# Cluster attention then MoE attention on one core: rows of the first pair written from PSUM, causal mask and maximum in one instruction, and a new order table

## The chip, the cores and the metric

The kernel runs on one core of one Trainium2 chip. The metric is the device time of one execution in microseconds (us), as the median of several runs; less is better. A core has five instruction queues that matter here: PE (TensorE, matrix products and transposes), ACT (ScalarE), DVE (VectorE), POOL (GpSimd) and SP, which issues all of the kernel's DMAs. Each engine runs its own queue strictly in order. PE writes to PSUM, of which the kernel uses eight banks of 128 x 512 float32; ACT and DVE read and write PSUM and SBUF, POOL works in SBUF.

## The reference, cut to what matters

```python
def _attn_ref(q, k, v, centroids):              # B=4, H=8, S=768, D=64, 16 centroids
    q_assign = np.argmax(np.einsum('bhsd,hcd->bhsc', q_n, c_n), axis=-1)   # normalised
    k_assign = np.argmax(np.einsum('bhsd,hcd->bhsc', k_n, c_n), axis=-1)
    mask = q_assign[:, :, :, None] == k_assign[:, :, None, :]
    scores = np.where(mask, scale * np.matmul(q, k.transpose(0, 1, 3, 2)), -1000000000.0)
    ...                                          # softmax, then times v

def _moe_ref(x, w_gate, wq, wk, wv, wo):         # x: B, S, 512; E=4 experts; top 2
    logits = x @ w_gate
    topk = np.argpartition(-logits, K, axis=-1)[..., :K]
    ...                                          # w: softmax over the two chosen logits
    for e in range(E):
        q, k, v = x @ wq[e], x @ wk[e], x @ wv[e]
        causal = np.triu(np.ones((S, S), dtype=bool), 1)
        scores = np.where(causal, -1000000000.0, scale * (q @ k.transpose(0, 2, 1)))
        ...                                      # softmax a
        ye = a @ v @ wo[e]
        for kk in range(K):
            out += (topk[:, :, kk] == e)[..., None] * w[:, :, kk:kk + 1] * ye
```

Every query of the first part attends only to keys of its own cluster. The output of the first part, heads side by side, is the input x of the second, a causal attention per expert.

## The kernel before, in words

The work is cut into 24 sets. Sets 0 to 15 are pairs of heads of the cluster attention (four pairs for each of four batches); sets 16 to 23 are pairs of experts of the MoE attention, two for each batch. `K` and `Q` of a set are tiles `tk` and `tq` (three buffers each): for each of two heads, rows 0 to 63 hold the data split in a high and a low part of a float32, and the rows behind them extra rows that put a constant on the score. For a cluster set the rows 64 to 79 of K and Q are the **cluster rows**: a one-hot code of each token's cluster, on K's side scaled so that a key of another cluster gets minus 2^33. A product over 80 rows then gives scores that are already masked. Row 96 of Q holds minus the row maximum.

For a cluster set, `attention_operands` does: load q and k; PE transposes them (L531); PE multiplies them with the centroids `cbd` (L562), which are themselves made by `centroid_op` at the start (DVE's `cw`, L443; two transposes on PE, L449; a copy on ACT); PE transposes the result (L569); DVE makes the one-hot code `oh` in five instructions (L574, L575, L576, L581, L582); PE counts the clusters (L593); DVE drops with L600 those codes of q whose cluster no key has; PE transposes `oh` to rows (L607, into the bank `m4`); ACT scales them into the tile `rows` (L610); and two DMAs, `place_rows`, put them into K and Q. The product with `blk` on PE (L651) and DVE's L655, L659 and L663 zero the q of dropped codes. For the first set alone L655 and L659 write halves of Q directly instead of by DMA.

`core` then does, for each of two halves of the queries: the row scores (L978, PE, 80 rows, in float32), their maximum along the row (L988, DVE; partial maxima in `mx`, joined by L993), a transpose of the maxima (L1025 for the first set, L1004 otherwise) and a DMA or copy of them into row 96 of Q; then the transposed scores (L1059, L1060, PE), the exponential (L1065, ACT), the product with v (L1103, PE) and the sum of the exponentials for the norm, partly on POOL (L381) and partly on DVE (L382). For a MoE set the score tile of a query block ends with a 128x128 block on the diagonal: there DVE adds the mask `tri` to that block in PSUM (L986), and takes the maximum with L988. There are 96 such blocks, 12 in each of 8 sets, in tiles of 128 to 512 columns.

At the end of a MoE set the result of the product is copied from PSUM to a tile `avu` (two buffers; L376 on ACT or L377 on DVE), multiplied by the norm (`avu` by `rb`), copied as a high part into `kt` or `xk`, and the low part, `avu` minus `kt` or `xk`, is written to `qt` or `xq` (L381 on POOL or L382 on DVE). `moe_out` multiplies high and low part with the weights (L1213).

**What sets the order.** Each step is recorded as an operation, `op`, with a number. The table `SEQ` lists these numbers; `Plan.run` issues them in that sequence, so it fixes each engine's queue. A letter behind a number puts the operation on ACT, DVE or POOL instead of its first choice. `SLOT` fixes which of a tile's buffers each use takes. The durations and due times in `op(...)` play no part when the table is there. PE is kept busy at the start by matmuls of ones (`spin`, L1229).

## Time and profile before

| what | us |
|---|---|
| time, median of 3 runs | 701.75 (698.44 to 703.31) |
| the profiled execution's own time | 701.95 |
| span of the profiled execution, first to last instruction | 700.2 |
| mean granted TensorE clock | 0.996 of full speed |

The busy times are in rows 1 below. A stage is a stretch of the span: the start until the first row scores (about 21 us), the cluster stage to about 400 us, then the MoE stage, and a tail from 675 us. The chain of waits follows the work back from the last instruction to what released it; shares in it are shares of the span. A span counts as busy for PE whether the matmuls run at full clock or not, so the granted clock has to be read beside it.

### The profile page before, as it was taken

The page shows a single profiled execution, that of the slowest core. Times are in us where ns is not written, and L with a number is a line of the kernel's source. Part 1 is how long each engine was busy: PE and PEld are TensorE (multiplying, and loading weights), DVE is VectorE, ACT ScalarE, POOL GpSimd, SP SyncE. Part 2 cuts the span into 40 slices and gives each one's busy share as a digit, 9 for nine tenths or more (in the row PEclk, how much of TensorE's full clock was granted, in tenths as well). Part 3 has the DMA queues.
Part 4 walks back from the last instruction along what each step waited for, and adds up shares of the span by engine and source line. Part 5 has one row for each costly group of instructions (what it writes and reads, how often), then busy time and mean ns, then how long its engine had stood idle before and what let it go on. Part 6 is the DMA issues. An engine that isn't in the chain of part 4 may idle for free.

```text
span 700.2 us, 13106 instructions
## 1 busy us (share of the span) xinstructions
PE 680.8 (97%) x4523; PEld 526.6 (75%) x4523; DVE 554.7 (79%) x1215; ACT 350.5 (50%) x863; POOL 345.5 (49%) x285
## 2 busy tenths in 40 slices
PE   8999999999999999999999999999999989999997
PEld 6778767767767767767767688879779877877876
DVE  6998798888899688989999977783887766467842
ACT  5447545645645735656746532543452344333653
POOL 4585647479656387575486516134322236242221
PEclk9999999999999999999999999999999999999999
DMA  8766759678665777687859744537455455554223
GB/s 231 197 149 157 182 130 239 145 163 236 174 157 147 190 188 196 164 199 180 172 136 252 172 115 123 152 117 172 107 130 129 100 138 153 124 131 122 87 85 121
DMA packets 78094, 109.64 MB, mean 157 GB/s; under 512 B 22432, under 2 KB 61516, under 8 KB 78028
## 3 DMA queue, kind: packets, MB, share of 16 engines
q1 hardware_dynamic: 78028, 108.81, 62.0%
q8 instruction: 36, 0.59, 0.4%
q14 instruction: 30, 0.25, 0.1%
HBM read 36.54 MB, written 12.91 MB: 71 GB/s over the span
## 4 chain that ended last, share of the span: by engine, by line
PE 81%; DVE 9%; DMA 4%; issue 2%; ACT 1%; POOL 1%; SPq 1%; DVEq 0%; ACTq 0%; POOLq 0%
PE ps L1103 20%; PE ps L978 12%; PE ps L1059 11%; PE ps L1060 11%; PE ps L764 9%; PE ps L1213 5%; PE ps L816 4%; DVE mx L988 3%; PE ps L531 2%; PE ps L1127 2%; DMA tq<-mr 1%; DVE oh L582 1%; PE ps L562 1%; SPq L369 1%; DMA vt<-x 1%
## 5 line engine op out<-in xcount | busy, mean ns | idle before, releaser
L988 DVE TENSOR_REDUCE mx<-ps 128x1 f32<-128x384 f32 (+1 forms) x448 | 223.1, 544 | 24.6 <-PE ps L978 22.5
L1059 PE MATMUL ps<-tq,tk 128*128 128x384 f32 (+2 forms) x528 | 178.4, 341 | 1.2 <-ACT p L1065 1.2
L1060 PE MATMUL ps<-tq,tk 97*128 97x384 f32 (+2 forms) x528 | 173.7, 332 | 1.1 <-DMA tq<-mr 1.0
L1065 ACT ACTIVATE p<-ps 128x384 f32<-128x384 f32 (+2 forms) x288 | 119.2, 461 | 64.8 <-PE ps L1060 39.3
L978 PE MATMUL ps<-tk,tq 80*128 80x384 f32 (+4 forms) x512 | 144.9, 353 | 4.2 <-ACT avu L376 1.9
L1059 PEld LDWEIGHTS ps<-tq,tk 128*128 128x128 f32 x528 | 100.3, 190 | 10.3 <-issue 3.8
L978 PEld LDWEIGHTS ps<-tk,tq 80*128 80x128 f32 x512 | 89.4, 190 | 21.7 <-issue 9.1
L1060 PEld LDWEIGHTS ps<-tq,tk 97*128 97x128 f32 x528 | 100.6, 191 | 2.7 <-DMA tq<-mr 1.8
L381 POOL TENSOR_TENSOR acc<-acc,p 128x768 f32<-128x768 f32 (+2 forms) x37 | 58.2, 1574 | 63.3 <-DVE acc L382 26.2
L1070 POOL TENSOR_SCALAR_AFFINE_SELECT p<-p 128x256 f32<-128x256 f32 x48 | 21.6, 466 | 76.2 <-ACT p L1065 57.1
L1065 ACT ACTIVATE xl<-ps 128x384 f32<-128x384 f32 x88 | 40.7, 497 | 26.3 <-PE ps L1060 26.0
L1103 PE MATMUL ps<-p,vt 128*64 128x384 f32 x288 | 50.7, 491 | 0.0
L986 DVE TENSOR_TENSOR ps<-ps,tri 128x128 f32<-128x128 f32 x96 | 28.1, 292 | 22.4 <-PE ps L978 22.3
L381 POOL TENSOR_TENSOR acc<-p,p 128x768 f32<-128x768 f32 (+1 forms) x11 | 19.3, 1754 | 50.6 <-ACT p L1065 34.0
L376 ACT ACTIVATE hi<-ps 128x384 fp32r<-128x384 f32 x38 | 18.6, 492 | 48.6 <-PE ps L764 38.9
L1103 PE MATMUL ps<-p,vm 128*64 128x384 f32 (+2 forms) x288 | 41.5, 423 | 0.0
L1065 ACT ACTIVATE xh<-ps 128x384 f32<-128x384 f32 x80 | 37.8, 498 | 5.2 <-PE ps L1060 4.7
L382 DVE TENSOR_TENSOR acc<-acc,p 128x768 f32<-128x768 f32 (+2 forms) x33 | 26.8, 811 | 14.8 <-POOL acc L381 7.7
L1103 PEld LDWEIGHTS ps<-p,vt 128*64 128x64 f32 x288 | 19.6, 136 | 23.7 <-issue 21.4
L1178 POOL TENSOR_TENSOR xt<-avu,rb 128x384 f32<-128x384 f32 x26 | 26.6, 1035 | 15.7 <-DMA rb<-rd 15.7
L988 DVE TENSOR_REDUCE M<-ps 128x1 f32<-128x512 f32 (+3 forms) x64 | 31.4, 491 | 2.2
L1103 PEld LDWEIGHTS ps<-p,vm 128*64 128x64 f32 x288 | 18.5, 136 | 19.1 <-issue 13.5
(271 smaller groups left out, 1447.6 us busy)
## 6 DMA issues: line engine op xcount, KB each, us to landing
tq<-hi SPq DMA_DIRECT2D x88, 192.0 KB
tk<-hi SPq DMA_DIRECT2D x60, 192.0 KB
tk<-lo SPq DMA_DIRECT2D x46, 192.0 KB
rb<-rd SPq DMA_DIRECT2D x46, 192.0 KB
tq<-lo SPq DMA_DIRECT2D x45, 192.0 KB
vt<-in_v_dram SPq DMA_DIRECT2D x16, 384.0 KB
x<-xt SPq DMA_DIRECT2D x16, 384.0 KB
tk<-hi SPq DMA_DIRECT2D x16, 384.0 KB
```

The lines of the kernel that those rows point to most:

```text
L381: ways = [("pool", t_pool(n), lambda: POOL.tensor_tensor(dst(), a(), b(), op=fn)), ("dve", t_dve(n), lambda: DVE.tensor_tensor(dst(), a(), ...
L382: ("dve", t_dve(n), lambda: DVE.tensor_tensor(dst(), a(), b(), op=fn))]
L764: PE.matmul(m()[:, :HW], w_()[:, dc, es], x_[dc]()[:, c], start=(i == 0), stop=(i == 3 * DC - 1))
L816: PE.matmul(m()[:, :NV], x_[dc]()[:, ts], w_()[:, dc, :], start=(i == 0), stop=(i == 3 * DC - 1))
L978: PE.matmul(ps()[:, :w], Q[0:R, 0, h, c * 128:(c + 1) * 128], K[0:R, 0, h, i * w:(i + 1) * w], start=True, stop=True)
L986: DVE.tensor_tensor(e, e, tri, op=OP.add)
L988: DVE.tensor_reduce(to, ps()[:, :w], axis=AX.X, op=OP.max)
L1059: PE.matmul(p()[:, o_:HW], K[:, 1, h, ks], Q[:, 1, h, qs], start=True, stop=False)
L1060: PE.matmul(p()[:, o_:HW], K[0:R, 0, h, ks], Q[0:R, 0, h, qs], start=False, stop=True)
L1065: ACT.activation(pt()[:, h, o_:HW], p()[:, o_:HW], AF.Exp, scale=SC)
L1103: PE.matmul(av()[h * 64:(h + 1) * 64, o_:HW], d["vv"](h, kc), pt()[:, h, o_:HW], start=(kc == 0), stop=(kc == nk - 1), tile_position=(0, 6 ...
L1213: PE.matmul(m(), a_()[:, ts], w_()[:, ep, :], start=(ep == 0 and i == 0), stop=(ep == EP - 1 and i == 2))
```

## The change

**The first set's rows.** For set 0 the codes of `oh` are laid out head by head, so that `m4` holds 16 rows together for each of K and Q and each head. For the first half of the tokens (384 columns) these rows go from `m4` into K (new L635, DVE, or L639, ACT) and into Q (new L642, ACT, or L644, DVE): four instructions of 16 x 384. The other halves go by four small DMAs. L600's two instructions of 96 columns become four of 48 (new L608). `blk` for set 0 becomes `blk0`, which is made at the start from a shift, `pj`, one more DVE instruction there; `blk` itself is made later.

**Mask and maximum.** `tri` becomes 512 columns wide: 384 of zeros (one more memset on DVE) and the old triangle. A diagonal tile of w columns gets one `tensor_tensor_reduce`: sum of the tile and the last w columns of `tri`, written back to PSUM, and its maximum. In the queue it stands as two rows, the operation and a read of the accumulator (both new L1018). Other tiles keep the plain maximum (new L1020).

**The table.** `SEQ` and `SLOT` are new throughout. The gate's small tiles `gt` and `gs` take the tags `oh` and `sm`. Counts change little: PE 3320 to 3321 rows, DVE 1195 to 1188, ACT 855 to 866, POOL 270 to 276, SP 399 to 393.

```diff
 SEQ = """
-0 39 1 48 2 221 3 245 230 4 5 33 34 44 63 40 45 49 41 42d 389 46 37 50 51 38 47 68 6 52 7 43 54 66 55 8 9 67 10 56
...
-    tri = consts.tile([128, 128], BF)
-    DVE.tensor_scalar(tri, jp, 0.0, -BIG, op0=OP.is_gt, op1=OP.mult)
+    tri = consts.tile([128, 512], BF)
+    DVE.memset(tri[:, :384], 0.0)
+    DVE.tensor_scalar(tri[:, 384:], jp, 0.0, -BIG, op0=OP.is_gt, op1=OP.mult)
...
+    pj = sb.tile([128, 2, 128], I32, name="p1_0")
+    DVE.tensor_scalar(pj, pi, 4, None, op0=OP.arith_shift_right)
...
-        DVE.tensor_tensor(blk, pi, di, op=OP.is_equal)
+        DVE.tensor_tensor(blk0, pj, di, op=OP.is_equal)
...
         def ohg():
+            if n == 0:
+                return oh().rearrange("p a (i g c) -> p (a i) g c", i=2, c=NK)
...
-            for par in range(2):
+            for h in range(4 if n == 0 else 0):
+                w, cnt = oh()[:, :, h * NK:(h + 1) * NK], m3()[:, None, h // 2 * NK:(h // 2 + 1) * NK]
+                DVE.scalar_tensor_tensor(w, cnt.to_broadcast([128, HC, NK]), 1.0, w, op0=OP.min, op1=OP.mult)
+            for par in range(2 if n else 0):
...
+        for h in range(0 if n else 2):
+            def go_d(h=h):
+                DVE.tensor_scalar(K[64:64 + NK, 0, h, :HW], m4()[64 + 32 * h:64 + 32 * h + NK, :HW], BIG, -BIG,
+                                  op0=OP.mult, op1=OP.add)
...
+            half_row[h].append(op("dve", t_dve(HW), go_d, c2 + 6.6, [o4] + free, [m4], alt=("act", t_act(HW) + 0.18, go_a)))
+            half_row[h].append(op("act", t_act(HW), lambda h=h: ACT.activation(
+                Q[64:64 + NK, 0, h, :HW], m4()[32 * h:32 * h + NK, :HW], AF.Copy), c2 + 6.7, [o4] + free, [m4],
...
+            def place(T, i, h=h):
+                r = 64 * i + 32 * h + NK
+                return lambda: dma(T[64:64 + NK, 0, h, HW:], rows()[r:r + NK])
+            need_row.append(op("sp", [(0.64, 0.25)], place(K, 1), c2 + 7, [o_r] + free, [rows]))
+            need_row2.append(op("sp", [(0.64, 0.25)], place(Q, 0), c2 + 15, [o_r] + free, [rows]))
...
-                PE.matmul(m()[:, :HW], blk[:, h], rows(), start=True, stop=True)
-            o = op("pe", t_mm(HW), go, due, [o_r], [m, rows])
+                PE.matmul(m()[:, :HW], (blk if n else blk0)[:, h], rows(), start=True, stop=True)
+            o = op("pe", t_mm(HW), go, due, [o_r] + ([blk_ready] if n == 1 else []), [m, rows])
...
-        t, s, wt = tmp("gt", (128, 3, NC, E)), tmp("gs", (128, 6, NC)), tmp("wt", (128, E, NC))
+        t, s, wt = tmp("oh", (128, 3, NC, E)), tmp("sm", (128, 6, NC)), tmp("wt", (128, E, NC))
...
+                    to = mx()[:, h, cc, i:i + 1] if nb == 2 else tops(h)[:, cc:cc + 1]
                     if moe and i == nb - 1:
-                        e = ps()[:, w - 128:w]
-                        DVE.tensor_tensor(e, e, tri, op=OP.add)
-                    to = mx()[:, h, cc, i:i + 1] if nb == 2 else tops(h)[:, cc:cc + 1]
-                    DVE.tensor_reduce(to, ps()[:, :w], axis=AX.X, op=OP.max)
+                        DVE.tensor_tensor_reduce(ps()[:, :w], ps()[:, :w], tri[:, 512 - w:], 1.0, -3.0e38, OP.add, OP.max, to)
+                    else:
+                        DVE.tensor_reduce(to, ps()[:, :w], axis=AX.X, op=OP.max)
```

Three places show what the table moves. The first is PE's queue at the start, where the transposes of set 0's k and q (L531, new L535) meet those of the centroids (L449, new L453, reading `avu`). Before:

```order
L531 MATMUL ps_168<-identf,kt_142 128x128 x3
L531 MATMUL ps_176<-identf,kt_142 128x128 x3
L531 MATMUL ps_182<-identf,qt_146 128x128 x3
L449 MATMUL ps_192<-identf,avu_72 128x128 x2
L531 MATMUL ps_197<-identf,qt_146 128x128 x3
```

With the change:

```order
L535 MATMUL ps_174<-identf,kt_146 128x128 x3
L453 MATMUL ps_182<-identf,avu_72 128x128 x2
L535 MATMUL ps_187<-identf,kt_146 128x128 x3
L535 MATMUL ps_194<-identf,qt_150 128x128 x3
L535 MATMUL ps_201<-identf,qt_150 128x128 x3
```

The transposes of the centroids move ahead by two places: three of the four groups for k and q now stand behind them, where one did.

The second is DVE's queue from the end of set 0's one-hot code to the zeroing of q (before L582 to L655; with the change L588 to L687); `xh` and `xk` there belong to the second set. Before:

```order
L582 TENSOR_TENSOR oh_268<-ps_227,sm_237 128x6x4x16
L377 COPY xh_0_257<-ps_241 128x384
L600 SCALAR_TENSOR_TENSOR oh_268<-ps_283,oh_268 128x3x32 x2
L382 TENSOR_TENSOR xh_0_298<-xh_0_257,xh_0_272 128x384
L377 COPY xk_308<-ps_245 128x384
L377 CAST hi_316<-ps_245 128x384
L655 TENSOR_TENSOR tq_103<-xq_195,ps_322 64x384
L659 TENSOR_TENSOR tq_103<-xq_195,ps_322 64x384
L663 TENSOR_TENSOR xq_195<-xq_195,ps_322 128x384
```

With the change:

```order
L588 TENSOR_TENSOR oh_269<-ps_232,sm_240 128x384
L608 SCALAR_TENSOR_TENSOR oh_269<-ps_281,oh_269 128x3x16 x4
L377 COPY xh_0_300<-ps_257 128x384
L635 TENSOR_SCALAR tk_106<-ps_302 16x384
L644 CAST tq_107<-ps_302 16x384
L687 TENSOR_TENSOR tq_107<-xq_205,ps_317 64x384
L691 TENSOR_TENSOR tq_107<-xq_205,ps_317 64x384
L695 TENSOR_TENSOR xq_205<-xq_205,ps_317 128x384
```

Two copies of the second set (`xk` and `hi`) and one subtraction left this stretch, and the two rows of set 0 that DVE writes itself stand in it.

The third is in the MoE stage, near 560 us of the trace, where a set ends: the subtraction that writes `xq` from `avu` and `xk`, and the copy of a later product into the same buffer of `avu` (its second buffer, `avu_1`). Before, the subtraction is on POOL, between additions to `acc`:

```order
L1070 AFFINE_SELECT p0_0_7424<-p0_0_7424 128x2x128
L381 TENSOR_TENSOR acc_0_7517<-p3_0_7380,p0_0_7424 128x2x256
L381 TENSOR_TENSOR xq_0_7520<-avu_1_6849,xk_0_7370 128x768
L381 TENSOR_TENSOR acc_1_7614<-p2_0_7433,p3_0_7556 128x768
L381 TENSOR_TENSOR acc_1_7614<-acc_1_7614,p0_0_7542 128x768
```

With the change the subtraction is on DVE:

```order
L1018 ISA M6_113 128x1
L1018 ISA ps_6_7373,M6_113<-ps_6_7373,tri_80 128x128
L1018 ISA M6_113 128x1
L1020 TENSOR_REDUCE mx_0_7375<-ps_3_7371 128x1
L382 TENSOR_TENSOR xq_0_7403<-avu_1_6942,xk_0_7331 128x768
```

The copy into that buffer is then on DVE too (before it was on ACT), 27 rows behind the subtraction:

```order
L1018 ISA ps_1_7491,M6_113<-ps_1_7491,tri_80 128x384
L1018 ISA M6_113 128x1
L377 COPY avu_1_7524<-ps_2_7514 128x384
L1020 TENSOR_REDUCE mx_0_7375<-ps_1_7526 128x1
L1018 ISA ps_6_7535,M6_113<-ps_6_7535,tri_80 128x512
```

Over the MoE stage's seven such subtractions of qt and xq, POOL has five before and one with the change; the others are DVE's.

## Rows read from the trace of the kernel before

**Rows 1.** Two lines of the profile's page: the busy time of each engine (share of the span, number of instructions), and the chain that ended last, by engine.

```profile
PE 680.8 (97%) x4523; PEld 526.6 (75%) x4523; DVE 554.7 (79%) x1215; ACT 350.5 (50%) x863; POOL 345.5 (49%) x285
...
PE 81%; DVE 9%; DMA 4%; issue 2%; ACT 1%; POOL 1%; SPq 1%; DVEq 0%; ACTq 0%; POOLq 0%
```

**Rows 2.** Busy time by stage: the start, the rest of the cluster stage, the MoE stage, the tail. Columns: from:to (us), length, busy us and instructions of each engine, granted TensorE clock, share of the DMA engines, GB/s.

```profile
0.00:21.00 21.00, 18.17 (x138) 13.00 (x138) 15.58 (x46) 9.88 (x20) 10.38 (x20) 1.00 0.82 221
21.00:400.00 379.00, 372.15 (x2479) 273.15 (x2480) 336.90 (x686) 217.90 (x518) 240.12 (x164) 1.00 0.73 178
400.00:675.00 275.00, 269.55 (x1777) 224.21 (x1776) 194.25 (x469) 113.59 (x308) 91.45 (x98) 0.99 0.49 126
675.00:700.00 25.00, 20.93 (x134) 16.20 (x132) 8.02 (x16) 9.09 (x18) 3.53 (x4) 0.97 0.31 111
```

**Rows 3.** The chain that ended last, from the start to 27 us. Columns: start us, us, what.

```profile
7.02 0.28 PE ps L449 x2
7.30 0.33 PE ps L531 x3
...
16.17 0.55 DVE tq L655
...
18.96 0.55 DVE xq L663
...
22.84 2.65 DVE mx L988 x6
...
25.80 0.57 PE ps L1025 x3
```

**Rows 4.** The timeline from 13 to 21 us. Columns: start us, us, engine, line, operation, out<-in.

```profile
13.48 0.58 DVE L377 COPY xh<-ps 128x384 f32<-128x384 f32 x1
...
15.69 0.44 PE L651 MATMUL ps<-rows,blk 128*128 128x384 f32 x1
15.70 0.62 SPq L369 DMA_DIRECT2D tk<-rows  x1
...
16.41 1.27 SPq L369 DMA_DIRECT2D tq<-rows  x1
...
20.93 0.41 PE L978 MATMUL ps<-tk,tq 80*128 80x384 f32 x1 [0.68 <-DMA qt<-in_q_dram]
```

**Rows 5.** The timeline from 2 to 7 us, the setup of constants on DVE and POOL. Columns as in rows 4.

```profile
2.19 0.33 DVE L425 TENSOR_SCALAR acc<-acc 128x256 int32<-128x256 int32 x1
...
2.44 0.76 POOL L467 MEMSET tk<- 64x768 f32 x1
2.45 0.90 DVE L426 TENSOR_SCALAR acc<-acc 128x256 int32<-128x256 int32 x1
...
3.27 0.21 DVE L434 SCALAR_TENSOR_TENSOR avu<-rb 128x64 f32<-128x64 f32 x1
...
6.11 0.73 DVE L443 TENSOR_SCALAR avu<-rb,nr 128x64 f32<-128x64 f32 x2
```

**Rows 6.** DVE's instructions grouped by line, operation and tile, over the whole span, a group for each shape. Columns: line, operation, out<-in, shapes, number, busy us, mean ns of one, idle before.

```profile
L600 DVE SCALAR_TENSOR_TENSOR oh<-ps,oh 128x96 bf16<-128x96 f32 x32 | 6.9, 261 | 1.1 <-PE ps L593 0.8 <-issue 0.2
...
L395 DVE MEMSET avu<- 128x256 f32 x1 | 0.3, 272 | 0.0
...
L434 DVE DVE_READ_ACCUMULATOR avu<-rb 128x1 f32 x1 | 0.1, 78 | 0.0
```

**Rows 7.** The same view of DVE, for the mask, a row maximum of 512 columns, and a product of 384 columns with one input in PSUM.

```profile
L986 DVE TENSOR_TENSOR ps<-ps,tri 128x128 f32<-128x128 f32 x96 | 28.1, 292 | 22.4 <-PE ps L978 22.3
...
L663 DVE TENSOR_TENSOR xq<-xq,ps 128x384 f32<-128x384 f32 x30 | 15.7, 547 | 3.4 <-PE ps L651 3.3
...
L988 DVE TENSOR_REDUCE M<-ps 128x1 f32<-128x512 f32 x16 | 11.1, 692 | 0.5
```

**Rows 8.** What DVE waited for from 400 to 700 us. Columns: engine, tile, line, what it waited for: us in total, times, longest us.

```profile
DVE ps L986 <- PE ps L978: 22.3, 19, 5.2
```

**Rows 9.** The same view of what PE waited for from 400 to 700 us.

```profile
PE ps L1004 <- DVE M L993: 0.7, 1, 0.7
```

**Rows 10.** Busy time in 2 us windows around 562 us, columns as in rows 2.

```profile
560.00:562.00 2.00, 0.11 (x2) 0.04 (x1) 1.93 (x4) 0.58 (x2) 1.39 (x1) 1.00 0.98 252
562.00:564.00 2.00, 2.00 (x6) 1.84 (x7) 1.93 (x6) 1.66 (x5) 0.00 (x0) 0.51 0.64 143
564.00:566.00 2.00, 2.00 (x10) 1.62 (x9) 0.66 (x2) 0.49 (x3) 0.00 (x0) 0.64 0.01 3
```

**Rows 11.** The chain that ended last, 559 to 563 us, columns as in rows 3.

```profile
559.63 1.77 POOL xq L381
...
561.42 0.50 ACT avu L376
...
561.96 0.65 PE ps L978
```

**Rows 12.** One instruction of DVE in the timeline from 559 to 562 us, columns as in rows 4.

```profile
559.79 1.63 DVE L853 TENSOR_TENSOR gt<-gt,gs 128x24 f32<-128x24 f32 x1
```

**Rows 13.** DVE's instructions by shape: the subtraction of the MoE output's high part, and an addition of 128x768, both with two inputs in SBUF.

```profile
L382 DVE TENSOR_TENSOR wvh<-xl,xl 128x768 f32<-128x768 f32 x1 | 2.3, 2333 | 0.0
...
L382 DVE TENSOR_TENSOR xq<-avu,xk 128x768 fp32r<-128x768 f32 x1 | 1.0, 960 | 0.3 <-ACT xk L376 0.3
```

**Rows 14.** POOL's instructions by shape: the same subtraction there.

```profile
L381 POOL TENSOR_TENSOR xq<-avu,xk 128x768 fp32r<-128x768 f32 x2 | 3.6, 1822 | 0.0
```

More of the change, by code (lines that the diff above doesn't have):

```diff
@@ L222 @@
+    vt="110000010101010100101010100110",
+    mx="0101010101101001100110101001011001010101",
     ssb="01010101010101010101010",
[L223 removed]
+    acc="010101010101010101010110101010100101",
     avu="010101010101010101010101",
     r="0101010101010101010101010",
[L226 removed]
+    xt="0100100110100010010010101001011010110",
     mr="01010101010101010101010",
[L228 removed]
+    vm="011010110101",
     lg="0101",
[L230 removed]
+    g="01230123",
@@ L1233 @@
     cbd_ready = centroid_op()
+    blk_ready = op("dve", 0.33, lambda: DVE.tensor_tensor(blk, pi, di, op=OP.is_equal), base(0) + 10, at=4.9)
     POOL.memset(MZ, 0.0)
```

379 lines of the change are left out of this document (195 added, 184 removed), and 6 rows, old and new, of the table SEQ.

## The prediction

> **What bounds the kernel now.** I read the busy times and the engines' shares of the chain first. PE is busy for 680.8 of 700.2 us, and 81% of the chain is PE; DVE holds 9% of it, though it is busy for 79% of the span [rows 1]. So an instruction saved on DVE is worth its time only where PE waits for it, and the next view has to say where PE is idle. By stages PE is idle for 2.83 of the first 21 us, 6.85 of the next 379, 5.45 of the 275 of the MoE stage, and 4.07 of the tail [rows 2]. That is all there is to win without taking work off PE, and the change takes none off. DVE is idle for 275 − 194.25 = 80.75 us of the MoE stage [rows 2].
>
> Then the chain at the start. Until 16 us it goes through PE (transposes, centroids) and DVE's one-hot code; from 16.17 us it lies on DVE alone: product and zeroing of q for two heads until 19.51, then the second pair's one-hot code, then six row maxima from 22.84 to 25.49, and only then PE again [rows 3]. The first row score starts at 20.93 [rows 4], some 2 us before DVE takes its maximum: the DMAs of the rows, which this change partly removes, are not what the chain waits for there.
>
> Then the one place in the MoE stage where PE stands still. [...] The chain there is POOL's subtraction `xq` (1.77 us), then ACT's copy into the `avu` that this subtraction reads, then a row score [rows 11].
>
> **The change part by part**, against the profiled execution's 701.95 us; that lies 0.2 above the median of the runs, 701.75.
>
> *Setup.* Two DVE instructions are added ahead of the centroids' norm, which starts right behind L426 on a full queue [rows 5]: a memset, at most the 0.27 us of one of 128x256 float32 [rows 6], and a shift of 128x256 integers, like L425 (0.33) or like L426 (0.90, while a POOL memset runs) [rows 5]. That is 0.60 to 1.17 us later for `cw`, or nothing if the load of the centroids is what the norm waits for. I take 0.6, since the norm started only as L426 ended. `cw` was done at 6.84 [rows 5], and its transposes began at 7.02 [rows 3], so there was 0.18 us in hand.
>
> *Transposes.* PE now takes the centroids' transposes second, with three groups of k and q behind them instead of one; a group took 0.33 and the centroids' pair 0.28 [rows 3]. They end at 6.84 + 0.6 + 0.28 + 3 × 0.33 = 8.71 instead of 7.63: +1.1. Bounds: 8.11 with no delay of `cw` (+0.5), 9.28 with 1.17 (+1.65). PE is in order, and nothing but ones stands there to fill the gap.
>
> *Strips.* Two instructions of 0.261 [rows 6] become four of half the columns. If the time went by columns alone, nothing is added; if not at all, 2 × 0.261 = 0.5. I take +0.2. The start is then +1.3 (bounds +0.5 and +2.15).
>
> *Rows from PSUM.* Two 16 x 384 instructions on DVE and two on ACT. Their bound is a 384-column instruction on DVE, 0.55 each [rows 7]. They go where DVE had the second pair's copies, in the time in which PE transposes, ACT makes `rows` and PE makes the first product at 15.69 [rows 4]; I cost them at nothing. If that cover were short, at most 1.1 us would be added. The gain is nothing too: the maxima still stand behind the second pair's one-hot code on DVE (the order's second place), so scores that come earlier only wait. What the DMA's share was in front of the first score is 20.93 − 16.72 = 4.2 us [rows 3, 4]; that is the first rival.
>
> *Mask and maximum.* 96 mask additions of 0.292 go [rows 7], and 96 accumulator reads come at 0.078 [rows 6]: 28.0 − 7.5 = 20.5 us less on DVE, if the joined instruction takes as long as the maximum did. Two rows speak for that: a product of 384 columns with one input in PSUM takes 0.547, and from the mask's 0.292 at 128 columns to a maximum's 0.692 at 512 it is 1.04 ns a column with 0.16 fixed [rows 7]. If instead it ran at half that rate, 31,744 columns (1,984 for each head of a set, 2 heads, 8 sets) would add 33 us, and DVE would do some 12.5 us more than now; the stage's 80.75 idle us cover that. On the path: DVE waits 22.3 us for scores before the mask [rows 8], so it is mostly ahead of PE here. PE waited for joined maxima once, for 0.7 us [rows 9]. I take −0.5; bounds: 0, and −1.5 if as much again goes elsewhere.
>
> [...]
>
> *Stall at 560 us.* PE lost 1.89 us there, and by the granted clocks 0.49 × 2 + 0.36 × 2 = 1.70 behind it [rows 10]: 3.6 in all. With the change that `xq` is on DVE, where it takes 0.96 instead of 1.82 [rows 13, 14], and it stands 27 rows ahead of the copy that waits for it, so POOL's queue (an addition to `acc` just ahead of it) no longer holds the copy. I take −3.6. What is late next there is DVE itself, which had its own queue full at 559 to 562 us [rows 10].
>
> *All else of the table.* PE's rows are the same work; DVE gets a few more subtractions in the MoE stage (six of seven instead of two), 4 × 0.96 = 3.8 us [rows 13], less than what the masks give back. I cost that at nothing.
>
> Sum: 701.95 + 1.3 − 0.5 − 3.6 = 699.15, so **699.2**. With all bounds of these terms: 701.95 + 0.5 − 1.5 − 3.6 = 697.35 to 701.95 + 2.15 − 3.6 = 700.5.
>
> **The rivals.**
>
> *The stall stays or moves* (702.75): 699.15 + 3.6. Two buffers of `avu`, in-order queues, and a new sequence: another wait of 2 us with its half clock behind it can arise at any of the seven set ends. For it: one such place was there, and the order alone doesn't tell when DVE reaches the subtraction. Against it: the stage has only one such place in 275 us. It also stands for the case that the table doesn't do what it seems to.
>
> *The start follows the rows* (695.0): if the first maxima could be taken as the first scores come, 4.2 us less: 699.15 − 4.2 = 694.95. For it: this is where the change puts the most new code. Against it: the chain from 16.17 to 25.5 is DVE's, and DVE's order there has the same work.
>
> *PE's idle time in the MoE stage goes* (695.7): all 5.45 us and the 1.70 of half clock instead of −0.5 and −3.6: 701.95 + 1.3 − 5.45 − 1.70 = 696.1, with setup at its lower bound 695.3; middle 695.7. For it: DVE has 20 us more room. Against it: DVE wasn't what most of these waits ended with [rows 9].
>
> *Subtractions on DVE held by POOL* (709.95, slower). Four subtractions with two inputs in SBUF move to DVE. An addition of 128x768 of that kind took 2.33 us once on DVE instead of 0.95 [rows 13], and an instruction of 24 columns with two inputs in SBUF took 1.63 us, from 559.79, while POOL's `xq` ran from 559.63 to 561.40 [rows 11, 12]. So DVE can be held as long as POOL's instruction lasts, and behind such a subtraction stand maxima and copies that PE waits for. If three of the four do to PE what happened at 560, at 3.6 each: 699.15 + 10.8 = 709.95. One is the first rival over again; it decides the sign from three on. Against it: POOL's five subtractions of 1.82 us leave, and such holding is there today without a stall of PE but one.
>
> [...]
>
> **How the numbers follow.** Chances: forecast 0.42, stall stays or moves 0.24, start 0.12, MoE idle 0.10, held subtractions 0.12. The likeliest is 699.2. The range from 693 to 706 takes in all but the last case and leaves room below for two of the gains together and above for a second stall (702.75 + 3.6 = 706.35). About 1% (7 us) is what a measurement of this kernel can tell from no change: 694.7 to 708.8. Faster by more: the start and MoE cases when they come with the low setup or together, 0.18 with a part of the forecast's lower tail. Slower by more: the held subtractions, 0.12. Within: 0.70.
>
> **What would show it.** Right: the centroids' transposes (new L453) begin at about 7.4 us and the first zeroing of q about 1.3 us later than 16.17; the joined instruction and its read together take about 0.77 us at 512 columns; the masks leave PE's share of the chain as it is; no window of the MoE stage has PE at 0.1 busy and a half clock. Wrong: a first transpose of the maxima much before 25.8 us (the rows did count); an idle PE before a copy into `avu` elsewhere (moved stall); DVE subtractions of 2 us ahead of late maxima (held). The cluster stage, where the table changes as much and for which I cost nothing, could prove the sum incomplete in either direction: its 6.85 us of PE idle bound the gain there, nothing bounds a loss.

## The result, and the profile after

The changed kernel takes 704.99 us (median of 16 runs, 701.04 to 710.74), the kernel before 701.08 (16 runs, 698.44 to 703.31). The ratio is 1.0059 with a 95% interval of 1.0038 to 1.0080: about 4 us slower, where 699.2 and a gain of 2.5 us had been forecast. By the 1% that a measurement was said to tell it is "no change", but the sign is beyond the interval. The runs of the changed kernel scatter twice as widely as those of the kernel before, and the profiled execution is the slowest of the 16, 710.74 us (span 709.0), so its losses are larger than those of the median run; e3 below shows one place where the scatter comes from. Ratios below are to runs of the kernel before on the same chip.

Two lines of the changed kernel's page, busy times and the engines' shares of the chain (compare [rows 1]):

```profile
PE 688.9 (97%) x4523; PEld 531.4 (75%) x4523; DVE 528.2 (74%) x1210; ACT 354.3 (50%) x873; POOL 354.3 (50%) x289
...
PE 81%; DVE 11%; DMA 3%; ACT 2%; issue 1%; SPq 0%; POOL 0%; DVEq 0%; ACTq 0%; POOLq 0%
```

Its busy times by stage, columns as in [rows 2]:

```profile
0.00:21.00 21.00, 17.03 (x111) 11.78 (x111) 12.45 (x43) 7.67 (x14) 12.36 (x23) 1.00 0.62 182
21.00:400.00 379.00, 370.36 (x2471) 271.49 (x2468) 327.12 (x671) 219.62 (x525) 251.51 (x170) 0.99 0.71 176
400.00:675.00 275.00, 272.50 (x1776) 225.90 (x1777) 176.69 (x476) 116.79 (x313) 83.82 (x91) 0.98 0.50 130
675.00:700.00 25.00, 23.89 (x151) 18.35 (x150) 11.26 (x22) 7.79 (x20) 6.64 (x8) 0.93 0.20 70
```

DVE works 17.6 us less from 400 to 675 us (176.69 for 194.25), and PE is idle there for 2.50 us instead of 5.45: that part of the plan came true. PE's share of the chain is the same 81%. The start lost (PE idle for 3.97 us instead of 2.83), and so did the rest of the cluster stage (8.64 instead of 6.85). The granted clock is lower in three stages: 0.99, 0.98 and 0.93 where it was 1.00, 0.99 and 0.97. Over the whole span PE is busy for 688.9 us instead of 680.8, with the same 4,523 instructions: by the profile most of the 8.8 us by which this span is longer than that of the kernel before are longer instructions of PE, not its waits.

What PE waited for, over the whole span: engine, tile, line, what it waited for, us in total, times, longest.

```profile
PE ps L1091 <- ACT xk L376: 2.6, 1, 2.6
...
PE ps L453 <- DVE p L448: 2.3, 1, 2.3
PE ps L1036 <- DVE M L1018: 1.7, 1, 1.7
PE ps L1092 <- DMA tq<-mr: 1.6, 1, 1.6
...
PE ps L928 <- DVE acc L382: 1.1, 1, 1.1
```

The kernel before had one wait above 1.5 us outside the start, the 1.9 us at 560 us [rows 10, 11]. That one is gone. In this execution four stand in its place: for ACT's `xk` (at 164 us), for DVE's maxima (at 523), for the DMA of the maxima `tq<-mr` (at 398) and for DVE's `acc` (at 689); and one in the start, for the centroids (the row names L448, but the transposes read `avu`, which L447 wrote until 7.66). By the traces of the experiments below they aren't equally firm. The one at 164 us is 2.5 us or more wherever it isn't repaired, and the one for `acc` 1.1 to 1.4 us wherever it isn't repaired, except in e1; the one at 398 us is 0.4 to 1.9 us long, and the one at 523 us, 1.7 us here, is at most 1.2 us elsewhere and mostly small or absent.

**The start.** The chain, columns as in [rows 3]:

```profile
7.68 0.69 PE ps L453 x2
8.37 1.92 PE ps L535 x9
...
11.14 1.44 PE ps L568 x8
...
14.02 0.57 DVE sm L580
...
18.36 0.68 ACT rows L621
...
19.07 0.02 DVEq L635
...
19.13 0.56 DVE tk L635
...
19.71 0.55 DVE tq L644
...
20.29 0.55 DVE tq L687
...
23.73 0.48 DVE sm L580
```

The centroids' transposes (new L453) start at 7.68 us, 0.66 later than before [rows 3]. But they take 0.69 instead of 0.28, and the three groups behind them 0.64 each instead of 0.33. By these durations PE runs at about half speed until past 13 us, and it did so ahead of its wait of 2.3 us as well: two groups of three, ahead of the wait and behind it, in the timeline, columns as in [rows 4]:

```profile
4.52 0.85 PE L535 MATMUL ps<-identf,kt 128*128 128x128 f32 x3
...
8.16 0.85 PE L535 MATMUL ps<-identf,kt 128*128 128x128 f32 x3
```

In the kernel before such a group takes 0.49 us from 7.13, and in the changed kernel it does so from 13.82. Both kernels begin slowly (16 products of ones in 3.6 us from 1.13; 12 of them take 1.47 us from 11.80 in the kernel before); the kernel before had sped up when the centroids came, and the changed kernel hadn't. The profile's row of the granted clock says 1.00 in all of this, and only the durations show it. The one-hot code, begun at 10.29 in the kernel before, begins at 14.02 here: 3.7 us later. Then ACT's `rows` and DVE's two rows of set 0 (new L635, L644) run one behind the other: the wait at 19.07 us is of DVE for ACT, though both read the bank and write different tiles. The second pair's code starts at 23.73 where it had started at 19.51 [rows 3].

**The stall at 164 us.** Four rows of the timeline from 155 to 167 us, columns as in [rows 4]:

```profile
158.38 0.52 ACT L376 ACTIVATE hi<-xq 128x384 fp32r<-128x384 f32 x1
...
158.93 2.96 SPq L369 DMA_DIRECT2D tq<-hi  x4
...
164.89 0.49 ACT L376 ACTIVATE hi<-ps 128x384 fp32r<-128x384 f32 x1 [5.99 <-DMA tq<-hi]
...
165.82 0.44 PE L1091 MATMUL ps<-tq,tk 128*128 128x384 f32 x1 [2.64 <-ACT xk L376]
```

ACT has copied q's high part into the tile `hi` at 158.38. Four DMAs read `hi`, issued from 158.93 on. The next instruction in ACT's queue writes `hi` again, with a later pair's k, and waits for those DMAs: ACT does nothing for 5.99 us, the exponentials stand behind it, and PE waits 2.64 us for a bank. The clock behind it, columns as in [rows 2]:

```profile
164.00:166.00 2.00, 0.18 (x1) 0.18 (x2) 0.56 (x1) 1.11 (x3) 2.00 (x2) 1.00 1.01 231
166.00:168.00 2.00, 2.00 (x10) 1.58 (x11) 0.00 (x0) 2.00 (x7) 2.00 (x2) 0.81 0.95 335
168.00:170.00 2.00, 2.00 (x8) 2.00 (x7) 1.02 (x2) 1.22 (x5) 0.05 (x1) 0.50 0.66 230
170.00:172.00 2.00, 2.00 (x11) 2.00 (x11) 0.58 (x2) 1.74 (x4) 0.48 (x1) 0.84 1.12 232
```

From 166 to 172 us PE loses a further (0.19 + 0.50 + 0.16) × 2 = 1.7 us to the half clock.

### The profile page after: what moved, and what is told of

Read it like the earlier page. It is cut to its first block, busy times and chain, and to the rows that moved or that the text cites. A ratio compares the mean times of both kernels' runs of the same rounds, so it can differ in the third digit from the quotient of the medians.

```text
span 709.0 us, 13154 instructions
## 1 busy us (share of the span) xinstructions
PE 688.9 (97%) x4523; PEld 531.4 (75%) x4523; DVE 528.2 (74%) x1210; ACT 354.3 (50%) x873; POOL 354.3 (50%) x289
## 4 chain that ended last, share of the span: by engine, by line
PE 81%; DVE 11%; DMA 3%; ACT 2%; issue 1%; SPq 0%; POOL 0%; DVEq 0%; ACTq 0%; POOLq 0%
PE ps L1135 19%; PE ps L1091 12%; PE ps L1010 11%; PE ps L1092 11%; PE ps L796 9%; PE ps L848 5%; PE ps L1245 5%; PE ps L535 2%; DVE mx L1020 2%; PE ps L1159 2%; DVE oh L588 1%; PE ps L568 1%; DVE ps L581 1%; DVE ps L582 1%; DVE acc L382 1%
## 5 line engine op out<-in xcount | busy, mean ns | idle before, releaser
L1020 DVE TENSOR_REDUCE mx<-ps 128x1 f32<-128x384 f32 (+1 forms) x416 | 208.4, 547 | 48.9 <-PE ps L1010 47.3
L1091 PE MATMUL ps<-tq,tk 128*128 128x384 f32 (+2 forms) x528 | 182.3, 348 | 3.1 <-ACT xk L376 2.6
L1092 PE MATMUL ps<-tq,tk 97*128 97x384 f32 (+2 forms) x528 | 175.9, 336 | 1.6 <-DMA tq<-mr 1.6
L1010 PE MATMUL ps<-tk,tq 80*128 80x384 f32 (+3 forms) x512 | 142.3, 350 | 0.0
L381 POOL TENSOR_TENSOR acc<-acc,p 128x768 f32<-128x768 f32 (+2 forms) x33 | 54.8, 1659 | 60.7 <-DVE acc L382 34.4
L1018 DVE CUSTOM_DVE_ANT_0 ps<-ps,tri 128x512 f32<-128x512 f32 (+4 forms) x96 | 47.0, 518 | 16.3 <-PE ps L1010 16.0
L1135 PE MATMUL ps<-p,vm 128*64 128x384 f32 (+2 forms) x288 | 43.7, 440 | 0.3 <-POOL p L1102 0.3
L1210 POOL TENSOR_TENSOR xt<-avu,rb 128x384 f32<-128x384 f32 x29 | 31.4, 1094 | 19.5 <-DMA rb<-rd 11.8
L382 DVE TENSOR_TENSOR acc<-acc,p 128x768 f32<-128x768 f32 (+2 forms) x37 | 32.8, 887 | 11.1 <-POOL acc L381 7.2
L376 ACT ACTIVATE avu<-ps 128x384 f32<-128x384 f32 x34 | 16.6, 488 | 40.4 <-PE ps L1135 36.1
```

Source lines behind the costliest of these rows:

```text
L376: return op("act", t_act(n, sbuf), lambda: ACT.activation(dst(), src(), AF.Copy), due, after, use, alt=("dve", t_dve(n), lambda: DVE.tenso ...
L381: ways = [("pool", t_pool(n), lambda: POOL.tensor_tensor(dst(), a(), b(), op=fn)), ("dve", t_dve(n), lambda: DVE.tensor_tensor(dst(), a(), ...
L382: ("dve", t_dve(n), lambda: DVE.tensor_tensor(dst(), a(), b(), op=fn))]
L1010: PE.matmul(ps()[:, :w], Q[0:R, 0, h, c * 128:(c + 1) * 128], K[0:R, 0, h, i * w:(i + 1) * w], start=True, stop=True)
L1018: DVE.tensor_tensor_reduce(ps()[:, :w], ps()[:, :w], tri[:, 512 - w:], 1.0, -3.0e38, OP.add, OP.max, to)
L1020: DVE.tensor_reduce(to, ps()[:, :w], axis=AX.X, op=OP.max)
```

## The experiments

Three theories were on the table. A: the late start is what was lost. B: the stalls in the middle and the tail. C: the joined mask and maximum costs time. Later came D, a stall that is taken away only moves the waiting on, and E, the new order needs the joined instruction.

**e1: the centroids' transposes back behind three groups.**

```diff
-... 41 252 37 43d 45 38 42 50 46d 396 52 51d 17 53 ...
+... 41 252 45 43d 42 50 46d 37 396 52 38 51d 17 53 ...
```

(37 is the pair of transposes on PE, 38 its copy on ACT; 41, 45, 50, 52 are the four groups of k and q.)

> The changed kernel with one move in its order: the centroids' two transposes on PE, and ACT's copy of them, stand fourth again, behind three of the four groups for k and q, as in the kernel before. Theory A (the start is what was lost: PE stands idle for 2.3 us for the centroids, and its transposes and products behind that take twice as long): PE has only one group left behind the wait, the first one-hot maximum starts at about 11.5 us instead of 14.02, and the time falls by about 2.5 us from 704.99, to 702.5. Theory B (the loss is the stalls in the middle and the tail, at 164, 398, 522 and 688 us, which depend on when DMAs land): the start moves as in theory A, but the time stays within 1 us of 705. Theory C (the joined mask and maximum costs time in the MoE stage): no change beyond 1 us either.

Measured: 703.08 us, ratio 1.0043 (1.0021 to 1.0066). In its trace the one-hot code starts at 11.42, as expected, and the six maxima at 24.51. The time fell by 0.16% (1.1 us) only, within the overlap of the intervals. Between A and B it decides little.

**e2: the integers out of the norm's way** (and `tri` made behind the norm).

```diff
-    DVE.tensor_scalar(pj, pi, 4, None, op0=OP.arith_shift_right)
-    DVE.tensor_scalar(pi, pi, 67, None, op0=OP.bitwise_and)
-    DVE.tensor_scalar(di, di, 6, None, op0=OP.arith_shift_right)
...
         DVE.tensor_scalar(nr[:, 1:2], nr[:, 1:2], 1e-30, None, op0=OP.max)
+        DVE.tensor_scalar(pj, pi, 4, None, op0=OP.arith_shift_right)
+        DVE.tensor_scalar(pi, pi, 67, None, op0=OP.bitwise_and)
+        DVE.tensor_scalar(di, di, 6, None, op0=OP.arith_shift_right)
         DVE.reciprocal(nr[:, 2:3], nr[:, 1:2])
```

> The changed kernel with its three integer instructions of the setup moved from ahead of the centroids' norm to the place where DVE waits for ACT's table load within it, and the mask's constant made behind it; the order table is the changed kernel's. Theory A: the centroids are ready at 5.7 us instead of 7.66 if the norm waited for DVE only; PE's idle time of 2.3 us shrinks below 0.5, the one-hot code starts near 10.8 instead of 14.02, and the time falls by about 3 us, to 702. If the load of the centroids is late, the norm starts little earlier than 4.10 and the gain is below 1 us. Theory B and theory C: the time stays within 1 us of 705.

Measured: 705.90 us (6 runs), ratio 1.0085 (1.0054 to 1.0116). A miss. The three instructions took until 5.57 us and ACT's table load (1.28 us) with its activation until 4.71, so the centroids came at 7.0 us and not at 5.7; the one-hot code started at 12.41, 1.6 us earlier than in the changed kernel, and the time was no better. Its interval overlaps that of the changed kernel; why 1.6 us of an earlier start don't show in it stays open. PE still waited 2.0 us for the centroids. Ahead of that wait a group of three took 0.52 us here; behind it PE was at about half speed (two groups took 1.28 us from 7.64), and in this trace the row of the granted clock shows it, columns as in [rows 2]:

```profile
8.00:10.00 2.00, 2.00 (x13) 1.30 (x15) 1.82 (x3) 0.83 (x2) 1.86 (x3) 0.50 0.82 250
```

**e3 and e4: the joined instruction, out of the new order and into the old.**

```diff
# e3, in the changed kernel
-                        DVE.tensor_tensor_reduce(ps()[:, :w], ps()[:, :w], tri[:, 512 - w:], 1.0, -3.0e38, OP.add, OP.max, to)
-                    else:
-                        DVE.tensor_reduce(to, ps()[:, :w], axis=AX.X, op=OP.max)
+                        e = ps()[:, w - 128:w]
+                        DVE.tensor_tensor(e, e, tri[:, 384:], op=OP.add)
+                    DVE.tensor_reduce(to, ps()[:, :w], axis=AX.X, op=OP.max)
```

```diff
# e4, in the kernel before
-                    if moe and i == nb - 1:
-                        e = ps()[:, w - 128:w]
-                        DVE.tensor_tensor(e, e, tri, op=OP.add)
...
+                    if moe and i == nb - 1:
+                        DVE.tensor_tensor_reduce(ps()[:, :w], ps()[:, :w], tri[:, 512 - w:], 1.0, -3.0e38, OP.add, OP.max, to)
+                    else:
+                        DVE.tensor_reduce(to, ps()[:, :w], axis=AX.X, op=OP.max)
```

In e4 the wide `tri` is made behind the norm, and the gate's tiles share buffers as in the changed kernel.

> The changed kernel with the mask's addition and the maximum as two instructions again, in the changed order. Theory A and theory B: DVE works 20 us more in the MoE stage beside its idle time, and the time is the same or up to 1 us longer, 705 to 706. Theory C: the joined instruction is dearer on the path than the pair, and the time falls by 2 us or more, to 703 or less.

> The kernel before, in its own order, with the joined mask and maximum alone (and the two small tiles of the gate under other tags, for room). Theory A and theory B: 0 to 1 us less than the kernel before, 700.1 to 701.1. Theory C: 2 us or more above it, 703 or more.

Measured: e3 711.19 us (4 runs), ratio 1.0158 (1.0131 to 1.0185), 7 us slower than with the joined instruction; e4 699.20 us, ratio 0.9995 (0.9977 to 1.0013), no change. C falls. What no theory had is e3's size: the same edit is worth nothing in one order and 1% in the other. A mask and a maximum of 512 columns in the kernel before, and the joined instruction, its read and the next instruction in the changed kernel, timelines, columns as in [rows 4]:

```profile
555.82 0.29 DVE L986 TENSOR_TENSOR ps<-ps,tri 128x128 f32<-128x128 f32 x1
556.14 0.69 DVE L988 TENSOR_REDUCE M<-ps 128x1 f32<-128x512 f32 x1
```

```profile
448.31 0.69 DVE L1018 CUSTOM_DVE_ANT_0 ps<-ps,tri 128x512 f32<-128x512 f32 x1
448.92 0.14 DVE L1018 DVE_READ_ACCUMULATOR2_ANT M<- 128x1 f32 x1
448.92 0.55 DVE L1020 TENSOR_REDUCE mx<-ps 128x1 f32<-128x384 f32 x1
```

The read begins 0.08 us before the joined instruction ends, and the next instruction starts with it. From the first start to the last end the pair takes 1.01 us and the joined instruction with its read 0.75. Over the whole span DVE is busy for 531.9 us in e4 and was for 554.7 in the kernel before: 22.8 us less.

e3's trace also shows why runs scatter. The stall at 398 us, in the changed kernel and in e3, columns as in [rows 2]:

```profile
398.00:400.00 2.00, 0.43 (x2) 0.36 (x2) 2.00 (x5) 0.00 (x0) 2.00 (x3) 0.83 0.62 183
400.00:402.00 2.00, 2.00 (x7) 2.00 (x7) 0.04 (x2) 0.84 (x2) 2.00 (x2) 0.50 0.75 192
402.00:404.00 2.00, 2.00 (x8) 2.00 (x8) 0.99 (x2) 1.47 (x4) 0.56 (x1) 0.50 1.08 328
404.00:406.00 2.00, 2.00 (x8) 2.00 (x7) 0.00 (x0) 0.76 (x2) 0.00 (x0) 0.50 1.08 222
```

```profile
398.00:400.00 2.00, 0.35 (x2) 0.02 (x1) 2.00 (x5) 0.00 (x0) 2.00 (x2) 1.00 0.63 197
400.00:402.00 2.00, 1.92 (x11) 1.88 (x12) 0.84 (x3) 1.18 (x3) 2.00 (x3) 1.00 0.68 117
402.00:404.00 2.00, 2.00 (x13) 2.00 (x12) 0.47 (x2) 2.00 (x5) 0.86 (x1) 1.00 1.05 366
```

The wait is 1.6 us long in the changed kernel and 1.7 in e3: behind it the changed kernel's PE runs for nearly 7 us at half clock (a loss of 3.4 us), and e3's at full clock. In seven traces of this order the wait is 1.6 to 1.9 us long; half clock follows it in four (the changed kernel, e1, e2, e7: 0.50 to 0.55 in the lowest window of 2 us) and full clock in three (e3, e10, e11: 1.00). Whether a stall of this length costs itself or two to three times itself differs from run to run.

**e5: a subtraction moved in the kernel before** (with the joined instruction); 3344 writes `xq` of set 19.

```diff
-... 3343 3730 ... 3716 3344p 3596 ...
+... 3343 3344 3730 ... 3716 3596 ...
```

> The kernel before in its own order with the joined mask and maximum, and one operation moved: the subtraction xq that ended in the stall at 560 us is on DVE, right behind the copy that it needs. Theory A (a PE stall costs its length and the half clock behind it): PE no longer waits for ACT's copy into avu at 560 us, and the time falls by about 3.6 us from the same kernel with that subtraction on POOL, 699.2, to 695.6. Theory D (a stall only moves the waiting to the next place, since PE's order has other limits close behind): the stall goes but the time falls by less than 1.5 us.

Measured: 700.27 us, ratio 1.0002 (0.9983 to 1.0022). It says nothing on A or D, since it was the wrong subtraction: in its trace POOL's `xq` still runs from 557.96 to 559.73, ACT's copy waits for it, and PE's 1.9 us are there. The one at 560 us is set 17's, 3047 (e9). As a control it shows that moving another of the kind brings nothing.

**e6, e7, e8: start and stall repaired in the changed kernel, apart and together.** The start: e1's move; two of e2's three instructions where they were put there, the third and `tri` behind the norm; `blk` made later; and the four rows of set 0 on ACT. The stall: the copies that wait for `hi`, and the product that needs their bank, behind other work.

```diff
# e6, the rows (63 is rows on ACT, 69 and 65 K's rows, 66 and 70 Q's; a suffix sets the engine)
-... 63 69 7 66d 230 74 83 241 24 84 19 65a ...
+... 63 7 230 74 83 241 24 84 19 69a 66 65a ...
# e7 (1276, 1272, 1271: copies of set 7's k; 1028: the product; 1045 to 1048, 1040: exponentials)
-... 1276d 1272 1271 1045 1064 1083 1048 1028 1279 1282 1054 1280 1160 1042 1040 1158 1055 ...
+... 1045 1064 1083 1048 1279 1282 1054 1280 1160 1042 1040 1158 1276d 1272 1271 1028 1055 ...
```

> The changed kernel with its start repaired in three ways together: the centroids' transposes fourth on PE again; two of the three integer instructions where DVE waits for ACT's table load, the third and the mask's constant behind the norm; and the first pair's four rows all on ACT, behind the copies of the second pair, so that DVE's zeroing of q isn't behind them. Theory A: the centroids are ready at about 6.5 us, PE's transposes and products run at full speed, the first six maxima start at about 22.8 us instead of 27.1, and the time falls by about 4 us from the changed kernel, to 1.0000 of the kernel before (ratio 1.0059 for the changed kernel). Theory B (the stalls at 164 and 398 us decide): the start moves as said, but the stalls take some of it back; ratio 1.004 or more.

> The changed kernel with one stretch of its order changed, near 162 us: three copies of a later pair's k, which wait until four DMAs have read the tile hi, stand behind five exponentials and two copies that stood behind them, and the score product that needs their bank stands behind them too. Theory A and B: ACT isn't held for 6 us there, PE's stall of 2.6 us goes with the half clock behind it, and the time falls by 3 to 4 us from the changed kernel, to a ratio of 1.001. Theory D: the waiting goes to the next place, and the ratio stays above 1.004.

> Both repairs in the changed kernel. If start and stall add up (theories A and B): ratio 0.995, some 3.5 us faster than the kernel before. Theory D: 1.000 or more.

Measured: e6 701.57 us, ratio 1.0010 (0.9987 to 1.0034); e7 701.19 us, 1.0018 (0.9991 to 1.0046); e8 698.23 us, 0.9975 (0.9955 to 0.9994). From the changed kernel's 1.0059 the start is worth 0.49% (3.4 us), the stall 0.41% (2.9 us), and both 0.84% (5.9 us): they add up, as A and B together say, and D doesn't hold for them. Each difference of two ratios is uncertain by some 0.3% (2 us): e7's interval alone still overlaps that of the changed kernel, e6's and e8's don't. e6's start, in the chain from the start, is that of the kernel before:

```profile
8.33 1.04 PE ps L566 x8
...
10.52 0.57 DVE sm L578
...
22.89 2.66 DVE mx L1018 x6
```

and in e8 the stall at 160 us is 1.1 us long with the full clock behind it, columns as in [rows 2]:

```profile
160.00:162.00 2.00, 0.86 (x5) 0.55 (x4) 1.46 (x3) 1.89 (x6) 2.00 (x2) 1.00 0.92 200
162.00:164.00 2.00, 2.00 (x13) 1.98 (x12) 0.15 (x2) 1.34 (x5) 1.83 (x2) 1.00 0.95 344
```

**e9 and e13: the stall at 560 us in the kernel before,** with the joined instruction and without it. 3047 is the subtraction of set 17, 3046 the copy that it needs.

```diff
-... 3046d 3283 ... 3288 3047p 3435 ...
+... 3046d 3047 3283 ... 3288 3435 ...
```

> The kernel before in its own order with the joined mask and maximum, and the subtraction that does stand in front of the copy at 560 us (that of set 17; the run before moved the one of set 19, and the stall stayed) on DVE, right behind the copy that it needs. Theory A: PE's stall of 1.9 us goes with the half clock behind it, and the time falls by about 3 us from the kernel before, to a ratio of 0.996. Theory D (the waiting goes to the next place): ratio 0.999 or more.

> The kernel before with one operation moved and nothing else: the subtraction in front of the copy at 560 us on DVE, the mask and the maximum two instructions as before. If the gain of e9_before_xq_moved (ratio 0.9933) is the stall's alone: 0.993 to 0.995. If the joined instruction made the room on DVE for it: 0.997 or more.

Measured: e9 695.48 us (6 runs), ratio 0.9933 (0.9917 to 0.9950); e13 697.03 us (6 runs), 0.9946 (0.9931 to 0.9962). One operation of some 4,000, on another engine and earlier in the order, is worth 0.54% (3.8 us) by itself. e13 around 560 us, to be held against [rows 10]:

```profile
560.00:562.00 2.00, 2.00 (x12) 1.60 (x11) 1.93 (x6) 1.37 (x4) 0.00 (x0) 1.00 1.00 255
562.00:564.00 2.00, 2.00 (x11) 1.80 (x11) 1.93 (x6) 1.12 (x3) 0.00 (x0) 1.00 0.47 94
564.00:566.00 2.00, 2.00 (x14) 1.94 (x13) 1.17 (x4) 1.22 (x3) 1.68 (x1) 1.00 0.65 194
```

**e10: the tail.** In the changed kernel POOL multiplies `avu` by `rb` of set 22 while DVE adds to `acc`; two rows of its timeline, columns as in [rows 4], and the same two instructions in e10, where DVE does both:

```profile
687.88 1.83 POOL L381 TENSOR_TENSOR avu<-avu,rb 128x768 f32<-128x768 f32 x1
...
688.15 2.11 DVE L382 TENSOR_TENSOR acc<-acc,p 128x512 f32<-128x512 f32 x1
```

```profile
675.90 0.68 DVE L382 TENSOR_TENSOR acc<-acc,p 128x512 f32<-128x512 f32 x1
...
676.51 0.95 DVE L382 TENSOR_TENSOR avu<-avu,rb 128x768 f32<-128x768 f32 x1
```

```diff
-... 3930d 3660 3666d 3821p 3940 ...
+... 3930d 3660 3821 3666d 3940 ...
```

> Start and stall repaired as in e8_start_and_stall, and one operation of the tail moved from POOL to DVE: the product of avu and rb of set 22, which ran on POOL while DVE's addition of 512 columns with two inputs in SBUF took 2.1 us and PE waited 1.1 us for it. Theory A (DVE's addition is held by POOL's product): the addition takes 0.7 us, PE's wait goes with the half clock behind it, and the ratio falls from 0.9975 to 0.994. Rival (the product on DVE delays the output's low part by as much): the addition takes 0.7 us, but the ratio stays at 0.997 or more.

Measured: 695.79 us, ratio 0.9935 (0.9915 to 0.9954), 0.40% below e8 (the two intervals just miss each other). DVE's addition of 512 columns, 2.11 us beside POOL's product, takes 0.68 without it, and the product 0.95 on DVE instead of 1.83 on POOL. PE's wait of 1.1 us is gone, and with it the half clock behind it (0.68 and 0.50 in the two windows from 680 to 684 us in e8, 1.00 in e10). In the kernel before, DVE did this product (0.96 us from 681.82): it was the new table that gave it to POOL.

**e11: the joined instruction again, in the repaired kernel:** e3's edit, in e8.

```diff
-                        DVE.tensor_tensor_reduce(ps()[:, :w], ps()[:, :w], tri[:, 512 - w:], 1.0, -3.0e38, OP.add, OP.max, to)
...
+                        e = ps()[:, w - 128:w]
+                        DVE.tensor_tensor(e, e, tri[:, 384:], op=OP.add)
```

> Start and stall repaired as in e8_start_and_stall, with the mask's addition and the maximum as two instructions again. Theory E (the new order puts so much on DVE that it holds only with the joined instruction): 1% more than e8_start_and_stall, ratio 1.007, as e3_mask_apart was 1% above the changed kernel. Rival (the 1% of e3_mask_apart came with the late start or with the stall): less than 0.3% more, ratio 1.000 or less.

Measured: 704.57 us (6 runs), ratio 1.0068 (1.0045 to 1.0091), 0.93% above e8: E holds. PE's waits from 440 to 560 us in e11 (L1017 and L1018 are mask and maximum there, L1023 joins the partial maxima):

```profile
PE ps L1034 <- DVE M L1023: 0.7, 1, 0.7
PE ps L1133 <- DVE M L1018: 0.6, 1, 0.6
...
PE ps L794 <- DVE mx L1018: 0.3, 1, 0.3
```

e8 has no wait for a maximum there. DVE's busy time in that stretch is 88.5 of 120 us with the pair and 80.5 with the joined instruction: far from full in both, but behind at these places. The waits that the trace names come to 1.8 us there, and the span is 6.6 us longer than e8's (703.2 for 696.6): that DVE is late with maxima is shown, and that it makes all of the loss isn't.

**e12: two of the rows on DVE again,** in e8.

```diff
-... 63 7 230 74 83 241 24 84 19 69a 66 65a ...
+... 63 69 7 66d 230 74 83 241 24 84 19 65a ...
```

> Start and stall repaired as in e8_start_and_stall, with two of the first pair's four rows on DVE ahead of the zeroing of q, as in the changed kernel. Theory A (they stand on DVE's chain): the zeroing starts 0.8 us later, and so do the six maxima; ratio 0.9985. Rival (they go beside other work): the maxima start within 0.2 us of 22.9, ratio 0.9975.

Measured: 698.12 us, ratio 0.9969 (0.9952 to 0.9985), for e8's 0.9975. The trace does what A said (the maxima start at 23.61 instead of 22.9), and the time doesn't follow.

**e14 and e15: which part of the start.** e10 with the centroids' transposes second again (e14), and with the integers and `tri` ahead of the norm again (e15).

```diff
# e14
-... 41 252 45 43d 42 50 46d 37 396 52 38 51d 17 53 ...
+... 41 252 37 43d 45 38 42 50 46d 396 52 51d 17 53 ...
# e15, ahead of the norm (and taken out behind it)
+    DVE.memset(tri[:, :384], 0.0)
+    DVE.tensor_scalar(tri[:, 384:], jp, 0.0, -BIG, op0=OP.is_gt, op1=OP.mult)
...
+    DVE.tensor_scalar(pj, pi, 4, None, op0=OP.arith_shift_right)
+    DVE.tensor_scalar(pi, pi, 67, None, op0=OP.bitwise_and)
+    DVE.tensor_scalar(di, di, 6, None, op0=OP.arith_shift_right)
```

> All three repairs as in e10_tail_too, with the centroids' transposes second on PE again, as in the changed kernel. If the place of the transposes alone makes the late start: PE idles for about 1 us until the centroids are ready at 6.2 us, its transposes and products run at half speed behind that, the one-hot code starts 1.5 us or more later than 10.5, ratio 0.9955 or more. If it needs the late centroids too: the one-hot code starts within 0.6 us of 10.5, ratio 0.9935.

> All three repairs as in e10_tail_too, with the integer instructions and the mask's constant ahead of the centroids' norm again, as in the changed kernel. If the late centroids alone make the late start: ready at 7.66, the one-hot code starts at about 11.5 as in e1_cent_back, 1 us later, ratio 0.995. Rival (the second pair's work fills it): ratio 0.9935.

Measured: e14 696.64 us (6 runs), ratio 0.9935 (0.9919 to 0.9950); e15 697.43 us (6 runs), 0.9949 (0.9932 to 0.9966). The six maxima begin at 22.74 and 23.79 us. Neither alone makes the 4 us: with early centroids the new place of the transposes costs nothing, and with the old place late centroids cost 0.9 us in the trace. Only together do they leave PE idle for 2.3 us and slow until past 13 us; in e14, where PE is idle for 0.85 us from 5 to 7 us, the eight products with the centroids then take 0.89 us, and in e15, where it is idle for 1.16 us from 5 to 9 us, 1.04 (1.44 in the changed kernel).

## Why the prediction was wrong

**The setup and transposes: +1.3 forecast, about +4 in the trace, +3.4 in the time (e6).** This is one of the two terms that failed. The delay of `cw` was taken as 0.6 us and was 0.82 (6.84 to 7.66): nearly right. The step that failed is "0.28 + 3 × 0.33": the durations were taken from a PE at full speed. Measured are 0.69 + 1.92, so the transposes end at 10.29 and not at 8.71. Behind the wait that the sum itself contained (PE has nothing but the centroids to do) PE is at about half speed, and the ones and the products that follow take 1.4 to 1.8 times as long (eight products with the centroids 1.44 us for 1.04, four products of ones 1.06 for 0.60), until the one-hot code starts 3.7 us later. The prediction said of the stall at 560 us that the half clock behind it counts, and didn't apply the same to the wait that it was just adding. That PE ran at half speed behind such a wait is shown by e2's row of the granted clock (0.50 from 8 to 10 us, behind 2.0 us of idleness); in the changed kernel PE was slow ahead of the wait already (0.85 us for a group of three at 4.52) and hadn't sped up when it came.

**The strips: +0.2 forecast.** The four of 48 columns took 0.55 us (new L608, from 17.37 us), and two of 96 would take 2 × 0.261 [rows 6]: next to nothing is added. The other layout makes `oh` itself faster (new L588 took 0.56 us, L582 1.01), which the prediction didn't see.

**Rows from PSUM: nothing forecast.** In the trace they stand on the chain for 0.7 us (e12), in the time they cost nothing that these runs can tell. The nothing of the sum stands. The rival that the start follows the rows is refuted: the first scores come 0.4 us early in e6 (20.55 for 20.93), the six maxima don't (22.89 for 22.84), and DVE's chain sets the start there as before.

**Mask and maximum: −0.5 forecast, 20.5 us of DVE's work.** The work was forecast rightly: 22.8 us less (e4), and 0.75 us for the joined instruction with its read at 512 columns where 0.77 had been said. A read takes 0.142 us and not 0.078, but at least 0.08 us of it lies beside other work. On the path the edit is worth nothing in the old order (e4; 0.1%, within the intervals, between e13 and e9) and 0.9 to 1.0% in the new one (e3, e11). The prediction costed the edit in the old order's profile and added it to the new order; the two are one term, since the new order doesn't hold its time without the edit.

For the pair's 1.01 us at 512 columns the trace has 0.75 with the joined instruction; what that is worth in time depends on the order.

**The stall at 560 us: −3.6 forecast.** Right, in place, mechanism and size. It is gone in the changed kernel, and taken away alone it brings 0.54% (e13).

**"All else of the table: nothing".** The other term that failed, and the larger one in what it hid. The stall at 164 us costs 2.9 us (e7) and the one in the tail 2.8 (e8 to e10). The rival "the stall stays or moves" (702.75) was nearest: a stall stays, at two places that the repairs confirm (164 us and the tail), and in the profiled execution at two more (398 and 523 us) that no run repaired and whose price stays open. The tail is the case of the held-subtraction rival, with an addition in its place (2.11 us beside POOL's product, 0.68 without it) and one stall instead of three. The prediction saw that "nothing bounds a loss" in the cluster stage and still gave it no term. The pieces of the order that would have shown the stall were there to read: a copy into `hi` right behind the copy whose DMAs read `hi`, in ACT's queue. The rival that PE's idle time in the MoE stage goes came half true in the profiled execution (2.50 of 5.45 us are left), and the time didn't follow.

Together: +3.4 (start), +2.9 (164 us), +2.8 (tail), −3.8 (560 us), +0 (mask) is +5.3 us for 4 measured. With some 2 us of uncertainty in each of the differences the sum agrees, and it can't say more: the waits at 398 and 523 us could be hidden in it.

**A version that beats both:** e9, the kernel before with the joined instruction and set 17's subtraction on DVE, 695.48 us, and e10, the changed kernel with its three repairs, 695.79. The two can't be told apart.

## What to carry to other kernels

When an order is rewritten, read on each engine's queue what is overwritten just behind the DMAs that read it, and what stands behind a wait that the change makes longer; here each of these cost about 3 us. A wait of PE is priced with the slower clock that can follow it (here 1.7 us behind the 2.6 us at 164 us, 3.4 behind the 1.6 us at 398, and nothing behind the 1.7 us there in e3), also a wait that one adds oneself. An instruction saved on an engine that isn't full (DVE is busy for 64% of the changed kernel's MoE stage) is worth what the order makes of it (0.1% in the old order here, 0.9 to 1.0% in the new): measure the edit in the order in which it will run.

## What was not expected of the hardware

PE ran at about half speed from its first products to past 13 us, across 2.3 us of idleness in the start (transposes 0.64 for 0.33 us a group), while the row of the granted clock read 1.00; in e2, behind 2.0 us of idleness, the row did show it (0.50 from 8 to 10 us). A PE wait of 1.6 to 1.9 us at about 398 us was followed by half clock in four traces (0.50 to 0.55) and by the full clock in three (1.00). The read of an accumulator (0.142 us) began 0.08 us before its instruction ended and together with the next one. And an ACT and a DVE instruction that only read one PSUM bank ran one after the other (L621 until 19.04, L635 from 19.13). DVE's idle time ahead of L635, 0.75 us, ends with ACT's L621 in the trace. So the rows that were given to two engines here didn't run side by side; what would happen without that wait no run shows.
